# Groups of 384 queries instead of 256 in a block-sparse attention with a gated convolution behind it

## The chip, the core and the metric

The kernel runs on one core of a Trainium2 chip. The time is device time of one execution in microseconds; lower is better. The core has a matrix engine (TensorE, PE in the profile, with its weight loads as PEld), a vector engine (DVE), an activation engine (ACT), a general engine (POOL) and a queue engine (SyncE, SP), which here issues nearly all DMAs. Each works through its own list in order and waits at semaphores.

## The reference

Four batches, eight heads, 768 positions, 64 numbers a head, all float32. A query sees the keys less than 16 positions away and, for each of the 24 blocks of 32 keys, one summary: the maximum of the keys and the mean of the values.

```python
k_sum = k.reshape(B, H, nb, block, D).max(axis=3)
v_sum = v.reshape(B, H, nb, block, D).mean(axis=3)
scores_l = scale * np.matmul(q, k.transpose(0, 1, 3, 2))
mask_l = np.abs(pos[:, None] - pos[None, :]) < window
scores_s = scale * np.einsum('bhsd,bhnd->bhsn', q, k_sum) + np.log(block)
a = softmax over both, with 1e-9 added to the sum
x = np.matmul(a, np.concatenate([v, v_sum], axis=2))       # heads side by side: 768 x 512
gate = sigmoid(sum over k of conv_w[k] * x shifted by k)   # causal, five taps
out = (gate * (x @ w_val)) @ w_out                         # two 512 x 512 matrices
```

## The kernel before

**Tiles and units.** Queries are taken in tiles of 64. A unit is one pair of heads and four such tiles (TPU), a group is the four units (four head pairs) of 256 queries (SG), and there are three groups (NTH) to a batch: 12 groups, 48 units. For a tile, 120 columns of keys stand side by side: 96 positions of the window and 24 block maxima; `v` has the same 120 rows, 96 from the window of `v` (three DMAs, L114) and 24 block means (`vs`, four DMAs of copies out of `vs`, `fill_vs`, L173).

**Stages of a unit.** `stage_s`: scores on PE (`s`, L293), mask and row maximum on DVE (L305), exponentials on ACT (`p`, L316). `stage_n`: reciprocal of the sums on DVE (`ri`), product on POOL (L328). `stage_t`: transposes on PE into one PSUM tile (`pt`, L337) and one copy on ACT (`pts`, L339). `stage_av`: product with `v` on PE (`x`, L351), copies on ACT (`xh` rounded for a fast matmul, `xf` whole), the rest `xl` on POOL, and the five taps of the convolution into PSUM on DVE (`g`, L377; the fifth tap on ACT, L370, in the early groups), then tanh on ACT (`gt`).

**Projections of a group.** `proj_val` (L397) multiplies x by w_val in three fast matmuls for each pair of 128-blocks (high by high, high by low, low by high); group 0, whose weights are not split yet, uses full float32 (L390). DVE gates the result (`gf`, L405), ACT and POOL split it into `gh` and `gl`, and `proj_out` (L419) multiplies by w_out, again in three; ACT scales it into `ob` and SP stores it. Weights and the convolution's coefficients come as 64-bit words and are made into float32 by ACT and DVE (`to_f32`, L186 to L193) and split by ACT and POOL (L228, L229).

**The order of the work.** The program goes by steps, one for each unit. In step s it writes the side work (loads, block maxima `ks` of the next batch's keys on DVE, sums of its values on POOL), then `stage_n` of unit s-1, `stage_av` of unit s-4, `stage_t` of unit s-3 and `stage_s` of unit s (LAG_N, LAG_AV, LAG_T), with pieces of the projections between them as PROJ_RATE allows. SP's list keeps this order; the lists of PE, DVE, ACT and POOL are set by a scheduler when the program is built, PE's from the fifth step on. Tables say at which step of a batch the next batch's keys are loaded (LOAD_K) and reduced (PREP_K), and in which order the first loads go out (LOADS). The keys have eight buffers, `v` and `q` two each. Each DMA takes the next of eight counters in turn, and its issue waits until the DMA eight places before it, the last user of that counter, has landed.

Of the kernel before, what the change touches and what calls it, by code (L numbers as in the profile page):

```python
# [52 lines left out]
def tile_attention_then_gated_conv(  # L53
# [56 lines left out]
    def load_v(g):  # L110
        b, th = divmod(g, NTH)
        t = ld.tile([KW, TPU, DM], F32, tag="v", name=f"v_{g}")
        for r0, r1, s0 in ((0, WIN, 0), (OFF_O, OFF_B, WIN), (OFF_N, KW, WIN + QT)):
            nc.sync.dma_start(t[r0:r1], vw[b, th, s0 : s0 + r1 - r0])  # L114
# [51 lines left out]
    def fill_vs(g):  # L166
        b = g // NTH
        src = vsum[b]
        vr = vtile[g].rearrange("p (t e) c -> p e t c", e=2)
        for e in range(2):  # L170
            for half in range(2):
                off = OFF_A if (e == half) else OFF_B
                nc.sync.dma_start(  # L173
                    vr[off : off + HB, e],
                    src[half * HB : half * HB + HB].unsqueeze(1).broadcast_to([HB, TPU // 2, DM]),
                )
# [156 lines left out]
    def stage_t(u):  # L333
        s = st[u]
        pt = ps_t.tile([P, TPU, P], F32, tag="pt", name=f"pt_{u}")
        for i in range(TPU):
            nc.tensor.transpose(pt[:KW, i, :], s["pn"][:, i, :], ident)  # L337
# [1 line left out]
        nc.scalar.copy(pts, pt[:KW])  # L339
# [42 lines left out]
    def proj_val(g, co):  # L382
# [5 lines left out]
        if g == 0:  # L388
            for ci in range(4):
                nc.tensor.matmul(  # L390
                    pp[:, :SG], wvf[:, ci, cs], G["xf"][:, ci, HALO:],
# [194 lines left out]
```

## Time and profile before

| | |
|---|---|
| median of 3 runs | 293.86 us (293.66 to 294.35) |
| the profiled execution, its time and its span | 295.11 us, 293.3 us |
| PE, DVE, ACT, POOL busy | 250.3, 218.0, 190.1, 155.0 us |
| mean granted TensorE clock | 0.971 |
| DMA | 43.46 MB, 47.7% of the 16 engines' time by the one queue of SP |

In the profile, "L351 x" is the operation of line 351 that writes tile x. A group's row gives count, busy time, mean ns of one, and the idle time before it with what ended it. In a row of the timeline or chain the first two numbers are start and length in us; "SPq" is SP's queue issuing a DMA, "DMA v<-vs" a DMA in flight. Records of PE's matmuls overlap, so their busy time is longer than what they cost back to back. A row of a stage gives its bounds and length, each engine's busy time, the granted clock, the DMA engines' busy share and GB/s.

### The profile page before, as it was taken

To read this page: it belongs to the slowest core of one execution; us is meant where nothing else is said; L and a number is where in the kernel's file an instruction comes from. 1 tells how busy PE (TensorE), PEld (TensorE's weight loads), DVE (VectorE), ACT (ScalarE), POOL (GpSimd) and SP (SyncE) were. 2 spreads that over 40 slices of the span, in tenths; PEclk is the share of its full clock that TensorE was granted. 3 is DMA by queue.
4 is the path that set the end of the run, shared out by engine and by line. 5 is a ranking of instruction groups with operands and counts; after the bars stand their busy time and mean duration, and the time that the engine had idled before them with its cause. 6 is when DMAs were issued, how large, how long until landed. Compare 5 with 4: busy or idle time off the path is not lost.

```text
span 293.3 us, 7550 instructions
## 1 busy us (share of the span) xinstructions
PE 250.3 (85%) x2592; PEld 200.8 (68%) x2592; DVE 218.0 (74%) x827; ACT 190.1 (65%) x686; POOL 155.0 (53%) x224
## 2 busy tenths in 40 slices
PE   1352856999989998979989889699999999999994
PEld 0231634677767775867766677589888887989893
DVE  1948789988679857756749988587898897876420
ACT  1436868857966975947955978377695877735231
POOL 0124346998677666455467578264465453723240
PEclk9999995599999999999999999979999999999999
DMA  7999690781484283660474476706335052202011
GB/s 221 385 242 303 177 368 4 211 305 55 111 254 160 70 207 125 165 200 3 116 235 169 133 235 172 230 0 160 123 104 141 2 152 93 75 0 75 0 74 72
DMA packets 15302, 43.46 MB, mean 148 GB/s; under 512 B 2592, under 2 KB 3360, under 8 KB 14112
## 3 DMA queue, kind: packets, MB, share of 16 engines
q1 hardware_dynamic: 15264, 42.98, 47.7%
q8 instruction: 21, 0.34, 0.5%
q14 instruction: 17, 0.14, 0.2%
HBM read 34.32 MB, written 6.29 MB: 138 GB/s over the span
## 4 chain that ended last, share of the span: by engine, by line
PE 43%; DMA 22%; SPq 13%; DVE 10%; ACT 7%; issue 2%; ACTq 0%
PE val L397 15%; PE out L419 13%; DMA k<-in_kT_dram 12%; SPq L173 7%; PE x L351 7%; PE s L293 4%; PE pt L337 4%; DMA v<-in_vw_dram 3%; DMA v<-vs 3%; SPq L114 3%; DVE g L377 3%; DMA qbd<-in_qT_dram 3%; ACT p L316 3%; DVE ks L121 2%; DVE k L131 2%
## 5 line engine op out<-in xcount | busy, mean ns | idle before, releaser
L377 DVE SCALAR_TENSOR_TENSOR g<-xf,cwt,g 128x256 f32<-128x256 f32 x192 | 93.2, 486 | 7.2 <-ACT g L370 3.7
L316 ACT ACTIVATE p<-sn,nm 128x120 f32<-128x120 f32 x192 | 74.1, 391 | 27.4 <-DVE nm L305 24.3
L397 PE MATMUL val<-xh,wv 128*128 128x256 f32 x352 | 75.2, 296 | 2.2 <-ACT xh L362 1.2
L328 POOL TENSOR_TENSOR p<-p,ri 128x480 f32<-128x480 f32 x48 | 48.5, 1011 | 33.1 <-DVE ri L326 20.9
L397 PEld LDWEIGHTS val<-xh,wv 128*128 128x128 f32 x352 | 57.6, 192 | 6.2 <-ACT xh L362 2.6
L419 PE MATMUL out<-wo,gh 128*128 128x512 f32 x192 | 60.8, 402 | 1.1 <-ACT ob L425 1.1
L365 POOL TENSOR_TENSOR xl<-xf,xh 128x256 fp32r<-128x256 f32 x44 | 32.4, 737 | 41.0 <-ACT xf L363 40.9
L397 PE MATMUL val<-xl,wv 128*128 128x256 f32 x176 | 50.6, 290 | 0.0
L293 PE MATMUL s<-k,qbd 64*64 64x120 f32 x768 | 37.8, 300 | 14.9 <-DVE nm L305 6.1
L407 POOL TENSOR_TENSOR gl<-gf,gh 128x256 fp32r<-128x256 f32 x48 | 35.0, 734 | 22.6 <-ACT gh L406 22.2
L305 DVE CUSTOM_DVE_ANT_0 sn<-s,mask 128x120 f32<-128x120 f32 x192 | 43.7, 275 | 4.2 <-PE s L293 3.9
L293 PEld LDWEIGHTS s<-k,qbd 64*64 64x64 f32 x768 | 23.9, 146 | 26.4 <-issue 11.8
L351 PE MATMUL x<-pts,v 120*64 120x64 f32 x768 | 34.4, 232 | 7.5 <-DMA v<-vs 3.5
L419 PEld LDWEIGHTS out<-wo,gh 128*128 128x128 f32 x192 | 34.2, 188 | 8.4 <-ACT ob L425 1.5
L351 PEld LDWEIGHTS x<-pts,v 120*64 120x64 f32 x768 | 27.3, 140 | 18.1 <-issue 4.6
L337 PE MATMUL pt<-ident,p 128*120 128x128 f32 x192 | 33.3, 299 | 5.3 <-ACT pts L339 3.9
L316 ACT ACTIVATION_READ_ACCUMULATOR p<-sn,nm 128x1 f32 x192 | 37.2, 194 | 0.0
L419 PE MATMUL out<-wo,gl 128*128 128x512 f32 x96 | 37.1, 400 | 0.0
L142 POOL TENSOR_TENSOR vT<-vT 128x384 f32<-128x384 f32 (+3 forms) x48 | 27.4, 577 | 18.1 <-DMA vT<-in_vT_dram 16.7
L397 PEld LDWEIGHTS val<-xl,wv 128*128 128x128 f32 x176 | 33.8, 192 | 1.0 <-issue 0.5
L380 ACT ACTIVATE gt<-g 128x256 f32<-128x256 f32 x48 | 18.7, 389 | 22.4 <-DVE g L377 22.1
L405 DVE SCALAR_TENSOR_TENSOR gf<-gt,val 128x256 f32<-128x256 f32 x48 | 19.7, 417 | 15.3 <-PE val L397 13.1
(44 smaller groups left out, 300.8 us busy)
## 6 DMA issues: line engine op xcount, KB each, us to landing
k<-in_kT_dram SPq DMA_DIRECT2D x16, 478.0 KB
vT<-in_vT_dram SPq DMA_DIRECT2D x16, 384.0 KB
v<-in_vw_dram SPq DMA_DIRECT2D x12, 512.0 KB
out_dram<-ob SPq DMA_DIRECT2D x24, 256.0 KB
qbd<-in_qT_dram SPq DMA_DIRECT2D x11, 512.0 KB
v<-in_vw_dram SPq DMA_DIRECT2D x24, 128.0 KB
v<-vs SPq DMA_DIRECT2D x48, 48.0 KB
raw_wv<-in_wv_dram SPq DMA_DIRECT2D x4, 512.0 KB
```

What stands on the lines that cost most here:

```text
L142: nc.gpsimd.tensor_tensor(dst, src[:, :, :n], src[:, :, n : 2 * n], ALU.add)
L293: nc.tensor.matmul(sp[64 * e : 64 * e + 64, h, j * KW : j * KW + KW], qbd[g % NQB][64 * h : 64 * h + 64, pr, i * QT : i * QT + QT], ktile[ ...
L305: nc.vector.tensor_tensor_reduce(sn[:, n, :], sp[:, h, j * KW : j * KW + KW], mask[:, mv, :], -1.0 / math.sqrt(D), 3.0e38, ALU.add, ALU.mi ...
L316: nc.scalar.activation(p[:, n, :], sn[:, n, :], AF.Exp, bias=nm[:, n : n + 1], scale=-1.0, accum_out=rs[:, n : n + 1],)
L328: nc.gpsimd.tensor_tensor(pn, s["p"], ri.unsqueeze(2).broadcast_to([P, TPU, KW]), ALU.mult)
L337: nc.tensor.transpose(pt[:KW, i, :], s["pn"][:, i, :], ident)
L351: nc.tensor.matmul(xp[h * D : (h + 1) * D, i * QT : (i + 1) * QT], v[:, i, c0 : c0 + D], s["pts"][:, 2 * (i // 2) + h, (i % 2) * QT : (i % ...
L365: nc.gpsimd.tensor_tensor(G["xl"][:, pr, :], x[:, pr, c0 : c0 + SG], G["xh"][:, pr, :].bitcast(F32), ALU.subtract)
L377: nc.vector.scalar_tensor_tensor(gt, x[:, pr, o : o + SG], cwt[:, pr, k : k + 1], gt, ALU.mult, ALU.add)
L397: nc.tensor.matmul(pp[:, :SG], w[:, ci, cs], G[x][:, ci, :], start=(n == 0), stop=(n == 11))
L407: nc.gpsimd.tensor_tensor(G["gl"][:, co, :], gf, G["gh"][:, co, :].bitcast(F32), ALU.subtract)
L419: nc.tensor.matmul(pp, G[gx][:, ci, si * P : si * P + P], w[:, ci, :], start=(n == 0), stop=(n == 11))
```

## The change

A group has 384 queries and a unit six tiles: NTH goes from 3 to 2, so there are 8 groups and 32 units. Each operation of a unit is half as wide again (128x384 for 128x256) or has six pieces for four. `stage_t` is written in two halves of three tiles, each with its own use of the one PSUM tile and its own copy, with a piece of the projections between the halves; the lags become 1, 2 and 3. PROJ_RATE and VAL_COST are half as large again, and the tables of steps are new. Buffers are shared: the keys of all pairs have six buffers under one name, with two of batch 0's value tiles in them; the float32 w_val lies in the buffers of `xh` and `xl`, the float32 w_out in those of `ob`; p, nm, rs, ri and pts have fewer. `v` is laid out in pieces of two tiles, 4096 bytes each, three to a row. The block means of group 0 are issued by ACT instead of SP.

```diff
-NTH = 3
+NTH = 2
+VP = TPU // 2
-LAG_N, LAG_T, LAG_AV = 1, 3, 4
-PROJ_RATE = 1.015
-VAL_COST, OUT_COST = 1.32, 2.6
-ACT_TAP_G = 5
-LOADS = "k0 q0 m k1 q1 n0 i k2 q2 n1 k3 q3 n2 n3 v0 c w0 w1 Q w2 w3"
+LAG_N, LAG_T, LAG_AV = 1, 2, 3
+PROJ_RATE = 1.52
+VAL_COST, OUT_COST = 1.98, 2.6
+ACT_TAP_G = 3
+LOADS = "k0 q0 m k1 q1 n0 i k2 q2 n1 k3 q3 n2 n3 v0 c w0 w1 w2 w3 Q"
-LOAD_K = ((6, 7, 8, 9), (1, 2, 8, 4))
-PREP_K = ((9, 10, 11, 11), (5, 8, 9, 8))
+LOAD_K = ((3, 4, 5, 6), (1, 2, 5, 6))
+PREP_K = ((5, 6, 7, 7), (3, 4, 7, 7))
...
     def load_k(b, pr):
-        t = ld.tile([P, KALLOC], F32, tag=f"k{pr}", name=f"k_{b}_{pr}")
+        t = ld.tile([P, KALLOC], F32, tag="k", name=f"k_{b}_{pr}", bufs=6)
...
-            nc.sync.dma_start(t[r0:r1], vw[b, th, s0 : s0 + r1 - r0])
+            src = vw[b, th, :, s0 : s0 + r1 - r0].rearrange("e r t c -> r e t c")
+            nc.sync.dma_start(t[r0:r1].rearrange("r (e t) c -> r e t c", e=VP), src)
...
     def fill_vs(g):
+        eng = nc.sync if g else nc.scalar
...
-                nc.sync.dma_start(
+                eng.dma_start(
...
-    wvf = cpool.tile([P, 4, DM], F32, tag="wvf", name="wvf")
+    wvf = [wk.tile([P, 2, DM], F32, tag=t, name=f"wvf_{t}") for t in ("xh", "xl")]
...
-            wof[k] = wk.tile([P, DM], F32, tag="wst", name=f"wst_{k}", bufs=2)
+            wof[k] = wk.tile([P, DM], F32, tag="ob", name=f"wst_{k}", bufs=2)
...
-        p = wk.tile([P, TPU, KW], F32, tag="p", name=f"p_{u}", bufs=4)
+        p = wk.tile([P, TPU, KW], F32, tag="p", name=f"p_{u}", bufs=3)
...
-    def stage_t(u):
+    def stage_t(u, half):
         s = st[u]
-        pt = ps_t.tile([P, TPU, P], F32, tag="pt", name=f"pt_{u}")
-        for i in range(TPU):
-            nc.tensor.transpose(pt[:KW, i, :], s["pn"][:, i, :], ident)
-        pts = wk.tile([KW, TPU, P], F32, tag="pts", name=f"pts_{u}", bufs=3)
-        nc.scalar.copy(pts, pt[:KW])
-        s["pts"] = pts
+        n = TPU // 2
+        if half == 0:
+            s["pts"] = wk.tile([KW, TPU, P], F32, tag="pts", name=f"pts_{u}", bufs=2)
+        pt = ps_t.tile([P, n, P], F32, tag="pt", name=f"pt_{u}_{half}")
+        for i in range(n):
+            nc.tensor.transpose(pt[:KW, i, :], s["pn"][:, half * n + i, :], ident)
+        nc.scalar.copy(s["pts"][:, half * n : half * n + n], pt[:KW])
...
+            if 0 <= s - LAG_T < NU:
+                stage_t(s - LAG_T, 0)
             carry = run_proj(carry + PROJ_RATE) if queue else 0.0
             if 0 <= s - LAG_T < NU:
-                stage_t(s - LAG_T)
+                stage_t(s - LAG_T, 1)
```

Three places of the lists show how the work moves. The rows name the line, the operation, what is written and read (tile names with a number, v_112 is group 0's `v`, v_304 group 1's), the shape, and the semaphores waited for; "DMAHW5" is one of the eight DMA counters. First ACT's list around the block means `vs` of group 0, before:

```order
L163 ACTIVATE vs_262<-vsp_257 24x512 [waits PE_49]
L316 ACTIVATE p_227,rs_229<-sn_226,nm_228 128x120 [waits DVE_49] x2
L339 COPY pts_285<-pt_280 120x512 [waits PE_49]
L186 ACTIVATE sc_cw<-cwraw 128x20 [waits DMAHW1_49]
L186 ACTIVATE sc_wv_137<-raw_wv_122 128x512 [waits DMAHW2_49]
```

and now:

```order
L190 ACTIVATE sc_wv_138<-raw_wv_123 128x512 [waits DMAHW2_49]
L166 ACTIVATE vs_298<-vsp_293 24x512 [waits PE_49]
L320 ACTIVATE p_255,rs_257<-sn_254,nm_256 128x120 [waits DVE_49] x3
L177 DMA v_112<-vs_298 12x3x512 [waits Activation_49]
L190 ACTIVATE sc_wv_143<-raw_wv_125 128x512 [waits DMAHW3_49]
L320 ACTIVATE p_255,rs_257<-sn_254,nm_256 128x120 [waits DVE_49] x3
L177 DMA v_112<-vs_298 12x3x512 [waits DMAHW5_49]
L177 DMA v_112<-vs_298 12x3x512 [waits DMAHW7_49]
L190 ACTIVATE sc_wv_148<-raw_wv_129 128x512 [waits DVE_49]
L177 DMA v_112<-vs_298 12x3x512 [waits DMAHW1_49]
L190 ACTIVATE sc_wv_191<-raw_wv_127 128x512 [waits DMAHW4_49,DVE_49,Activation_49]
L368 COPY xf_336<-x_322 128x384 [waits PE_49]
```

Four DMAs now stand in ACT's list between `vs` and the first copy of x, and three of them wait for a DMA counter. Which DMA stands behind a counter is seen in SP's list at that place, now (raw_wv_129 is the last weight, qbd_82 the second q, k_0_312 the first key tile of batch 1):

```order
L204 DMA raw_wv_129<-in_wv_dram 128x1024 [waits DMAHW5_49]
L99 DMA qbd_82<-in_qT_dram 128x1536 [waits DMAHW6_49]
L116 DMA v_304<-in_vw_dram 16x3x1024 [waits DMAHW7_49]
L116 DMA v_304<-in_vw_dram 64x3x1024 [waits DMAHW0_49]
L116 DMA v_304<-in_vw_dram 16x3x1024 [waits DMAHW1_49]
L177 DMA v_304<-vs_298 12x3x512 [waits DMAHW3_49,Activation_49]
L177 DMA v_304<-vs_298 12x3x512 [waits DMAHW4_49]
L177 DMA v_304<-vs_298 12x3x512 [waits DMAHW6_49]
L177 DMA v_304<-vs_298 12x3x512 [waits DMAHW0_49]
L103 DMA k_0_312<-in_kT_dram 128x956 [waits DMAHW2_49,DVE_49]
```

A DMA that waits for a counter takes that counter itself. So ACT's last three DMAs come behind the last weight (5) and the first and third piece of group 1's `v` (7 and 1), and k_0_312 comes behind ACT's first (2). Before, group 1's `v` was issued after all four copies of `vs` into group 0's.

Third, SP's list where a batch's first group is loaded, before (group 3, v_807):

```order
L114 DMA v_807<-in_vw_dram 16x2048 [waits DMAHW7_49,PE_49]
L114 DMA v_807<-in_vw_dram 64x2048 [waits DMAHW0_49]
L114 DMA v_807<-in_vw_dram 16x2048
L173 DMA v_807<-vs_836 12x2x512 [waits DMAHW2_49,Activation_49]
L173 DMA v_807<-vs_836 12x2x512 [waits DMAHW3_49]
L173 DMA v_807<-vs_836 12x2x512 [waits DMAHW4_49]
L173 DMA v_807<-vs_836 12x2x512 [waits DMAHW5_49]
L98 DMA qbd_81<-in_qT_dram 128x1024 [waits DMAHW6_49]
L426 DMA out_dram<-ob_0_924 128x512 [waits DMAHW7_49]
L426 DMA out_dram<-ob_1_968 128x512 [waits DMAHW0_49]
L102 DMA k_0_1002<-in_kT_dram 128x956 [waits DMAHW1_49]
```

and now (group 2, v_665):

```order
L116 DMA v_665<-in_vw_dram 16x3x1024 [waits DMAHW7_49,PE_49]
L116 DMA v_665<-in_vw_dram 64x3x1024 [waits DMAHW0_49]
L116 DMA v_665<-in_vw_dram 16x3x1024 [waits DMAHW1_49]
L177 DMA v_665<-vs_694 12x3x512 [waits DMAHW2_49,Activation_49]
L177 DMA v_665<-vs_694 12x3x512 [waits DMAHW3_49]
L177 DMA v_665<-vs_694 12x3x512 [waits DMAHW4_49]
L177 DMA v_665<-vs_694 12x3x512 [waits DMAHW5_49]
L99 DMA qbd_82<-in_qT_dram 128x1536 [waits DMAHW6_49,PE_49]
L103 DMA k_0_891<-in_kT_dram 128x956 [waits DMAHW7_49]
L108 DMA vT_0_893<-in_vT_dram 128x768 [waits DMAHW0_49,Pool_49]
L431 DMA out_dram<-ob_0_908 128x512 [waits DMAHW1_49,Activation_49]
```

The PE that the first row waits for is the last x of the group whose buffer is taken over. That x is written in the same step as the load before (step 4g+3 for both), and one step earlier now (4g+2). The rest of the list at this place is as it was, but for the stores, which come behind the first key tile.

More of the change, by code (lines that the diff above doesn't have):

```diff
@@ L38 @@
 HALO = NK - 1
+VP = TPU // 2
 REBIAS = 2.0 ** ((127 - 1023) // 8)
-LAG_N, LAG_T, LAG_AV = 1, 3, 4
-PROJ_RATE = 1.015
-VAL_COST, OUT_COST = 1.32, 2.6
-ACT_TAP_G = 5
-LOADS = "k0 q0 m k1 q1 n0 i k2 q2 n1 k3 q3 n2 n3 v0 c w0 w1 Q w2 w3"
-CONVERT = {"wv": (0, 0, 1, 0), "wo": (6, 9, 6, 11)}
-SPLIT = {"wv": (12, 4, 10, 5), "wo": (12, 9, 12, 12)}
-LOAD_K = ((6, 7, 8, 9), (1, 2, 8, 4))
-PREP_K = ((9, 10, 11, 11), (5, 8, 9, 8))
+LAG_N, LAG_T, LAG_AV = 1, 2, 3
[3 more added lines that the diff above has]
+LOADS = "k0 q0 m k1 q1 n0 i k2 q2 n1 k3 q3 n2 n3 v0 c w0 w1 w2 w3 Q"
+CONVERT = {"wv": (0, 0, 1, 0), "wo": (6, 7, 6, 6)}
+SPLIT = {"wv": (8, 3, 7, 4), "wo": (8, 7, 8, 8)}
+LOAD_K = ((3, 4, 5, 6), (1, 2, 5, 6))
+PREP_K = ((5, 6, 7, 7), (3, 4, 7, 7))
 PREP_V0 = (1, 2, 3, 3)
@@ L146, in load_vT0 @@
     def load_vT0(i):
-        t = ld.tile([P, S], F32, tag=f"k{i}", name=f"vT_0_{i}")
+        tag, n = (("k", 6), ("vT", 2))[i // 2]
+        t = ld.tile([P, S], F32, tag=tag, name=f"vT_0_{i}", bufs=n)
         nc.sync.dma_start(t, vT[0, i])
@@ L207, in staged @@
         if nm == "wv":
-            return wvf[:, k]
+            return wvf[k // 2][:, k % 2]
         if k not in wof:
-            wof[k] = wk.tile([P, DM], F32, tag="wst", name=f"wst_{k}", bufs=2)
+            wof[k] = wk.tile([P, DM], F32, tag="ob", name=f"wst_{k}", bufs=2)
         return wof[k]
@@ L284, in stage_s @@
         sn = wk.tile([P, TPU, KW], F32, tag="sn", name=f"sn_{u}")
-        p = wk.tile([P, TPU, KW], F32, tag="p", name=f"p_{u}", bufs=4)
-        nm = wk.tile([P, TPU], F32, tag="nm", name=f"nm_{u}", bufs=10)
-        rs = wk.tile([P, TPU], F32, tag="rs", name=f"rs_{u}", bufs=10)
-        for j in range(2):
+        p = wk.tile([P, TPU, KW], F32, tag="p", name=f"p_{u}", bufs=3)
+        nm = wk.tile([P, TPU], F32, tag="nm", name=f"nm_{u}", bufs=4)
+        rs = wk.tile([P, TPU], F32, tag="rs", name=f"rs_{u}", bufs=4)
+        for j in range(TPU // 2):
             for e in range(2):
@@ L299, in stage_s @@
                     )
-        for j in range(2):
+        for j in range(TPU // 2):
             for h in range(2):
@@ L323, in stage_n @@
         s = st[u]
-        ri = wk.tile([P, TPU], F32, tag="ri", name=f"ri_{u}", bufs=10)
+        ri = wk.tile([P, TPU], F32, tag="ri", name=f"ri_{u}", bufs=4)
         nc.vector.tensor_scalar(ri, s["rs"], 1e-9, None, ALU.add)
@@ L390, in proj_val @@
                 nc.tensor.matmul(
-                    pp[:, :SG], wvf[:, ci, cs], G["xf"][:, ci, HALO:],
+                    pp[:, :SG], wvf[ci // 2][:, ci % 2, cs], G["xf"][:, ci, HALO:],
                     start=(ci == 0), stop=(ci == 3),
@@ L534, in _layout @@
     vn[:, WIN : WIN + S] = v.transpose(0, 2, 1, 3).reshape(B, S, DM)
-    vw = np.zeros((B, NTH, QT + 2 * WIN, TPU, DM), f)
+    vw = np.zeros((B, NTH, VP, QT + 2 * WIN, 2, DM), f)
     for t in range(NT):
-        vw[:, t // TPU, :, t % TPU] = vn[:, t * QT : t * QT + QT + 2 * WIN]
+        i = t % TPU
+        vw[:, t // TPU, i // 2, :, i % 2] = vn[:, t * QT : t * QT + QT + 2 * WIN]
     cw = moe_conv_w.reshape(NK, NPR, 2 * D).transpose(2, 1, 0).reshape(2 * D, NPR * NK)
```

## The prediction

> **What bounds the kernel now.** I read the busy shares first, then three stages, then the chain of waits. Span and engines:
>
> ```profile
> core 0 of [0], span 293.3 us
> PE 250.3 (85%) x2592; PEld 200.8 (68%) x2592; DVE 218.0 (74%) x827; ACT 190.1 (65%) x686; POOL 155.0 (53%) x224
> ```
>
> Busy PE time counts overlapping records, so I price PE by what back-to-back matmuls take in the chain and in the timeline (start, us, line, count):
>
> ```profile
> 226.93 0.62 PE x L351 x16
> 231.93 0.57 PE s L293 x16
> 254.56 0.58 PE pt L337 x4
> 229.88 1.44 PE val L397 x12
> 222.27 4.11 PE out L419 x18
> 39.28 1.56 PE L390 MATMUL val<-xf,wvf 128*128 128x256 f32 x6 [1.85 <-ACT xf L363]
> ```
>
> One record each: x 0.039, s 0.036, pt 0.145, val 0.12, out 0.228, fp32 val 0.26. The program has 768, 768, 192, 528, 288 and 32 of them (counts of the groups): 29.8 + 27.4 + 27.8 + 63.4 + 65.8 + 8.3, with 1.6 for 16 small transposes 224.1 us. The last matmul ends near 289.3, so PE loses about 65 us. Where, the stage view says (length, busy of PE, PEld, DVE, ACT, POOL, clock, DMA share, GB/s), with s, pt, x and fp32 val before 60 us under it:
>
> ```profile
> 0.00:60.00 60.00, 33.54 (x295) 23.05 (x297) 45.36 (x162) 35.26 (x120) 25.98 (x31) 0.89 0.77 241
> 60.00:200.00 140.00, 127.57 (x1421) 101.82 (x1421) 108.04 (x437) 100.62 (x378) 89.04 (x139) 0.99 0.50 154
> 200.00:289.30 89.30, 89.22 (x881) 75.88 (x879) 64.63 (x229) 53.39 (x189) 40.03 (x54) 1.00 0.27 78
> 0.00:60.00 60.00, 9.90 (x160) 0.89 0.77 241
> 0.00:60.00 60.00, 7.32 (x32) 0.89 0.77 241
> 0.00:60.00 60.00, 3.95 (x66) 0.89 0.77 241
> 0.00:60.00 60.00, 12.06 (x32) 0.89 0.77 241
> ```
>
> Before 60: 5.7 + 4.6 + 2.6 + 8.3 + 0.6 = 21.8 us of work, 38 lost. From 200 on PE is full. Between them 224.1 - 21.8 - 89.3 = 113 of 140: 27 lost. So the kernel is a slow start, a middle with gaps, and a PE-bound end.
>
> The start, in the DMA rates of the first 30 us, the timeline and the chain:
>
> ```profile
> 0.00:10.00 10.00, 1.39 (x24) 1.05 (x28) 3.74 (x15) 2.27 (x6) 0.32 (x5) 1.00 0.80 269
> 10.00:20.00 10.00, 5.18 (x56) 2.95 (x48) 7.42 (x31) 4.45 (x22) 1.97 (x2) 1.00 1.05 277
> 20.00:30.00 10.00, 3.17 (x24) 2.11 (x24) 6.87 (x29) 5.58 (x17) 4.88 (x4) 1.00 0.99 310
> 4.05 0.95 DVE L121 TENSOR_REDUCE ks<-k 128x24 f32<-128x768 f32 x1 [4.05 <-DMA k<-in_kT_dram]
> 20.10 3.47 SPq L173 DMA_DIRECT2D v<-vs  x4
> 21.13 9.10 DMA v<-vs
> 31.73 0.91 PE L351 MATMUL x<-pts,v 120*64 120x64 f32 x12
> 33.53 0.49 DVE L377 SCALAR_TENSOR_TENSOR g<-xf,cwt,g 128x256 f32<-128x256 f32 x1 [0.23 <-ACT g L370]
> 59.94 0.69 PE L351 MATMUL x<-pts,v 120*64 120x64 f32 x16
> ```
>
> The means of group 0 are issued at 20.1, land 9 us later behind the weights, and hold the first x; its convolution starts at 33.5, and the fifth x runs at 59.94.
>
> The middle, in SP's waits and one turn of the chain:
>
> ```profile
> SPq L114 <- PE x L351: 116.5, 10, 16.8
> 99.02 0.64 PE x L351 x16
> 100.06 0.61 SPq L114
> 101.33 0.87 SPq L173
> 104.72 0.51 SPq L98
> 105.28 5.40 DMA k<-in_kT_dram
> 110.70 0.95 DVE ks L121
> 116.98 0.71 PE x L351 x16
> ```
>
> SP stands at a group's v load until the last x of two groups ago, then issues v, four means and q, and only then the k that DVE is about to reduce: 99.66 to 110.68, 11 us from x to the landed k. A q or a k stands so in the chain six times between 60 and 200 (from 81.49, 105.28, 123.29, 149.67, 167.98, 181.84): 27 / 6 = 4.5 us of PE lost at each.
>
> **The change part by part.** *PE work.* Per column val costs 0.12/256 and out 0.228/512; the line between gives 0.174 us at 384. 336 x 0.174 = 58.5 against 63.4: -4.9. Group 0 stays fp32 and is half as wide again: 32 x 0.39 against 8.3: +4.2. s, x, pt and out do the same count. Total 223.4: **-0.7**.
>
> *Helpers.* The rows are two sizes each for DVE and ACT, then from the chain one of the three operations of a weight's conversion and one S of a tile on DVE, and from the waits PE's for the copy of transposes:
>
> ```profile
> L377 DVE SCALAR_TENSOR_TENSOR g<-xf,cwt,g 128x256 f32<-128x256 f32 x192 | 93.2, 486 | 7.2 <-ACT g L370 3.7
> L405 DVE SCALAR_TENSOR_TENSOR gf<-gt,val 128x256 f32<-128x256 f32 x48 | 19.7, 417 | 15.3 <-PE val L397 13.1 <-POOL gl L407 1.0 <-POOL xf L273 0.4
> L190 DVE SCALAR_TENSOR_TENSOR wvf<-raw_wv,wvf 128x512 uint32<-128x512 uint32 x4 | 2.8, 691 | 0.0
> L363 ACT COPY xf<-x 128x256 f32<-128x256 f32 x48 | 18.0, 375 | 0.1
> L339 ACT COPY pts<-pt 120x512 f32<-120x512 f32 x48 | 28.2, 588 | 2.4 <-PE pt L337 2.2
> 39.66 0.70 DVE wst L190
> 41.68 0.19 DVE sn L305
> PE pt L337 <- ACT pts L339: 3.9, 3, 3.1
> ```
>
> DVE: (691 - 417)/256 = 1.07 ns a column, so 486 becomes 0.62 us. 128 x 0.62 against 93.2 is -14; gf, ri and the fifth tap give about -8: DVE near 196. ACT: (588 - 375)/256 = 0.83 ns, so 375 becomes 0.48; six copies or casts a unit save some 13 us over 32 units, the transposes in halves give 64 x 0.48 - 28.2 = +2.5 back. None of it is on the path while PE or the loads set the pace; it is slack, priced at 0, and worth up to what the middle loses.
>
> *Start.* Everything up to the weights and the second q is 7552 KB before (sizes of the issue list); with q of 192, v of 1152 and Q of 768 KB, and v_1 behind them, it is 9600 KB = 9.8 MB after. The three windows moved 8.56 MB by 30 us; 1.27 MB more at 310 is 4.1: v_1 lands at 34. The moved means matter for what they wait for: by the order, ACT's second, third and fourth wait for counters of the last weight, of v_1's first and of its last piece. So the fourth is issued at about 34, not 20, and at the 3 us which a small load takes (k, issued at 0.73, was there at 4.05) the first unit's x runs at **37** instead of 31.7. Queued behind that issue on ACT are two weight casts, xf, the tap, the copies of pt and the exponentials of unit 3; all wait. Four issues at SP's 0.8 are 3 us of ACT, inside that wait. On SP the same v_1 holds its fourth mean, then k_1_0; with 5.4 to land that is 40, and DVE has k_1_0's reduce ahead of unit 0's convolution: 40.5 against 33.5. From there to the fifth x lie, on DVE, three convolutions (4 x 0.62), four S (6 x 0.2), two k (0.95 and the two copies, 1.3), one and a half weight conversions (three operations, some 2.2) and 0.7 of ri: 19 us, at the 0.9 of the time that DVE is busy from 30 to 60, 21; with 3.5 for exponential, p, transpose and copy the fifth x runs near 65. PE work done then: 6.8 + 4.4 + 3.7 + 6.2 + 0.5 = 21.6, as before at 60. So the start costs **+5**. Below, -2 (means land early, the lighter DVE makes up for the rest); above, +12 (x at 40, and the ACT, PE and DVE waits add instead of overlapping).
>
> The page *DMA: Bandwidth & Descriptors* of the Trainium skill says (Queues, rings and completion order) that a DMA engine takes turns between the issuers' rings, so ACT's means pass SP's queued k and vT; its section on issuing engines says that a second issuer only saves issue time. By the first the sum stands; by the second k and vT (862 KB at 310, 2.8 us) go first and it would be about 3 higher. No row here shows a DMA issued by ACT.
>
> *Middle.* The last x of a group now lies one step before the v load instead of in its step. A step is 223.4/32 = 7.0 us, of the 11 that k was late. And only four v loads have k behind them (v_2 to v_5). If lateness and loss go together: 4 x 4.5 x (11 - 7)/11 = 6.5 us lost, the best. Against it: the means of a batch's first group wait for the block means, stores of out stand ahead of k_2_1, and a unit has two trips PE-ACT-PE through one PSUM tile where it had one; at worst the 27 stays. I take the middle, 16: **-11**.
>
> *End.* After the last x 21 val and 36 out remain by the order, 3.7 + 8.2 = 12 us of PE work; five taps (3.1), gt, gf, gh, gl and the copies need about 8. No gap: 0.
>
> Sum on the profiled span: 293.3 + 5 - 0.7 - 11 = 286.6. The median of the runs lies 0.6 above the span (293.86), though the profiled execution itself took 295.11. **Forecast: 287 us**, faster by 2%.
>
> **The rivals.** *ACT held at the start* (slower). The moved means wait for v_1, and everything behind them on ACT with them, ending at the fifth x near 72; the lost lead leaves k as late as now at two of the four places. 293.9 + 12 - 0.7 - 6 = **299**. For it: the waits in the order. Against: DVE has only 45 us of work in the first 60, so there is room to catch up. It decides when the fifth x comes later than about 71, 11 behind.
>
> *Two trips a unit* (no change). ACT is 65% busy and in order; where a gh or an exponential stands before the copy of the first half, PE waits at the second. PE already waited 3.9 us for that copy in all (three times), with one copy a step. The middle then loses 22: 293.9 + 5 - 0.7 - 5 = **293**.
>
> *The start costs nothing.* SP's loads are faster than in the windows or the means are not awaited so late, and the middle loses 10: 293.9 - 0.7 - 17 = **276**. For it: ACT, DVE and POOL all fall further below PE's 7.0 a step.
>
> **How the numbers follow.** Forecast 0.53, ACT held 0.24, two trips 0.11, start free 0.12. The forecast's own range is 280 to 293 (start +2 to +8, middle -6 to -16). The range of 80% reaches to the outer cases, leaving a tenth on each side: 275 to 301. Beyond 0.2% (which this kernel's runs can tell) faster: 0.53 + 0.12 = 0.65; same 0.05, out of two trips; slower 0.24 + 0.06 = 0.30.
>
> **What will show it.** Right: the first x near 37 with ACT idle before it on its own DMA issue; the fifth x near 65; SP's wait at the v load far below 116 us; fewer than six q or k on the chain from 65 to 200; val at 0.17 us apiece; PE full from some 190 on. Wrong start: first x by 32, or the fifth after 71. Wrong middle: as many k on the chain, or "ACT pts" among PE's first waits. If PE's work is much off 223, the pricing by columns is wrong.

## The result, and the profile after

The changed kernel takes **327.49 us** (median of four runs, 324.69 to 329.57), the kernel before 293.76 beside it on the same chip: a ratio of 1.112, 95% interval 1.100 to 1.123. It is 11% slower where 2% faster was forecast, and 26 us above the upper end of the range. (A ratio, here and below, leaves disturbed runs out on both sides and so can differ from that of the medians.) The profiled execution took 329.57 us, its span is 327.6.

The prices of the single operations came out as worked out. Groups of the page (count, busy time, mean ns of one, idle before), then from the timeline (start, us) a run of val and one of the fp32 val:

```profile
L382 DVE SCALAR_TENSOR_TENSOR g<-xf,cwt,g 128x384 f32<-128x384 f32 x128 | 79.4, 620 | 6.7 <-ACT g L375 3.4
L345 ACT COPY pts<-pt 120x384 f32<-120x384 f32 x64 | 31.0, 484 | 27.2 <-PE pt L344 27.2
```

```profile
242.40 2.10 PE val L402 x12
```

```profile
76.42 1.45 PE L395 MATMUL val<-xf,wvf_xl 128*128 128x384 f32 x4
```

So val is 0.175 us apiece and fp32 val 0.36, and PE's work is some 223 us by the counts, as before. What came on top is waiting, and in part a lower clock (last section). The stages of the changed kernel (bounds, length, busy of PE, PEld, DVE, ACT, POOL, clock, DMA share, GB/s), which answer to the prediction's three:

```profile
0.00:60.00 60.00, 22.99 (x255) 14.56 (x255) 35.93 (x129) 26.02 (x92) 17.50 (x24) 1.00 0.82 255
60.00:200.00 140.00, 124.63 (x1191) 92.39 (x1190) 101.03 (x363) 87.98 (x307) 84.02 (x105) 0.95 0.47 145
200.00:290.00 90.00, 83.72 (x761) 67.09 (x755) 50.25 (x193) 56.85 (x208) 34.55 (x34) 0.94 0.25 69
```

Busy time is too kind to PE, so for every kernel here I counted the matmuls that began in a stage, line by line, and multiplied by the prices (s 0.036, x 0.039, pt 0.144, out 0.228, val 0.119 at 256 and 0.175 at 384, fp32 val 0.26 and 0.36). What is left of the stage is lost:

| PE time lost, us | 0 to 60 | 60 to 200 | 200 to 290 | after 290 |
|---|---|---|---|---|
| before | 38.3 | 25.0 | 3.6 (0.8 of it behind its last matmul, which ends at 289.2) | |
| after | 44.2 | 33.9 | 17.6 | 3.2 to its last matmul, which ends at 322.1 |

The extra 33 us from one last matmul to the other are 6 at the start, 9 in the middle, 15 from 200 to 290 and 3 behind 290. (For before the prediction put the middle at 27, by difference; the count gives 25.)

*Start.* The timelines of PE, of ACT's queue and of two weight casts on ACT, and the chain:

```profile
37.66 0.48 PE L356 MATMUL x<-pts,v 120*64 120x64 f32 x4 [17.78 <-DMA v<-vs]
41.66 1.33 PE L356 MATMUL x<-pts,v 120*64 120x64 f32 x20 [3.51 <-DMA v<-vs]
71.81 0.84 PE L356 MATMUL x<-pts,v 120*64 120x64 f32 x10
```

```profile
25.00 1.40 ACTq L177 DMA_DIRECT2D v<-vs  x1
27.65 0.80 ACTq L177 DMA_DIRECT2D v<-vs  x1
32.81 0.79 ACTq L177 DMA_DIRECT2D v<-vs  x1
37.89 0.80 ACTq L177 DMA_DIRECT2D v<-vs  x1
33.65 0.66 ACT L190 ACTIVATE sc_wv<-raw_wv 128x512 f32<-128x512 f32 x1 [5.40 <-DMA v<-in_vw_dram]
38.82 0.66 ACT L190 ACTIVATE sc_wv<-raw_wv 128x512 f32<-128x512 f32 x1 [4.51 <-DMA v<-vs]
```

```profile
22.64 14.79 DMA v<-in_vw_dram
37.45 0.78 SPq L177
38.33 5.94 DMA k<-in_kT_dram
44.30 0.96 DVE ks L123
```

v_1's last piece lands at 37.4, ACT's fourth mean leaves right behind it, the rest of the first x runs at 41.7 and the fifth x at 71.8; before they were at 31.7 and 59.9. Two weight casts in ACT's list stood behind its third and fourth DMA for 9.9 us. (The profiled execution of the kernel before is a late one there: in the seven kernels below that are made from it and leave the first loads and group 0's means in their order, the first x begins at 27.8 to 28.8 us where it begins at 30.3, and the fifth at 56.0 to 58.6.)

*Middle.* One turn of the chain again, from the last x of a group to the landed k:

```profile
104.33 0.62 PE x L356 x14
105.36 0.67 SPq L116
106.71 0.84 SPq L177
...
110.70 8.27 DMA k<-in_kT_dram
118.99 0.95 DVE ks L123
...
139.44 0.62 PE x L356 x14
140.46 0.67 SPq L116
141.19 7.06 DMA v<-in_vw_dram
148.31 5.71 DMA k<-in_kT_dram
```

It takes 14.0 us where it took 11: 1.2 MB of v (0.8 before) are loaded ahead of k, and in the first turn 0.8 MB of q (0.5 before). The waits that stood out:

```profile
DVE ks L123 <- DMA k<-in_kT_dram: 27.3, 8, 5.8
ACT ob L430 <- DMA out_dram<-ob: 17.7, 5, 5.8
SPq L116 <- PE x L356: 92.8, 6, 26.5
```

SP stands 15.5 us at each v load where it stood 11.7, with a group half as long again. Of DVE's wait for k 6 us lie ahead of 10 us in both kernels; from 60 us on it is 20.7 us and was 10.0.

*End.* The chain and PE's timeline at 212 to 227:

```profile
212.92 0.67 SPq L116
214.33 0.82 SPq L177
...
218.30 7.50 DMA out_dram<-ob
225.82 0.61 ACT ob L430
```

```profile
226.47 1.22 PE L424 MATMUL out<-wo,gh 128*128 128x512 f32 x2 [2.91 <-ACT ob L430]
```

A group now has three stores of out and still two tiles for them. The stores stand on SP behind the v load, which waits for an x, and behind its means; then they fly together with v and q for 7.5 us. ACT's copy waits for the tile, and PE for ACT. At 253.6 the same happens once more.

### The profile page after: what moved, and what is told of

Read it like the earlier page. It is cut to its first block, busy times and chain, and to the rows that moved or that the text cites. A ratio compares the mean times of both kernels' runs of the same rounds, so it can differ in the third digit from the quotient of the medians.

```text
span 327.6 us, 6755 instructions
## 1 busy us (share of the span) xinstructions
PE 262.1 (80%) x2400; PEld 198.9 (61%) x2400; DVE 201.2 (61%) x707; ACT 183.2 (56%) x630; POOL 146.7 (45%) x172
## 4 chain that ended last, share of the span: by engine, by line
PE 37%; DMA 29%; DVE 13%; ACT 7%; SPq 5%; POOL 5%; issue 3%; ACTq 0%; POOLq 0%
PE out L424 15%; DMA v<-in_vw_dram 12%; DMA k<-in_kT_dram 10%; PE val L402 9%; DVE g L382 5%; PE x L356 5%; DMA out_dram<-ob 4%; PE pt L344 4%; ACT p L320 3%; PE s L297 3%; SPq L177 2%; DMA vT<-in_vT_dram 2%; DVE sn L309 2%; SPq L116 2%; DVE ks L123 2%
## 5 line engine op out<-in xcount | busy, mean ns | idle before, releaser
L332 POOL TENSOR_TENSOR p<-p,ri 128x720 f32<-128x720 f32 x32 | 44.9, 1404 | 90.4 <-DVE ri L330 63.9
L382 DVE SCALAR_TENSOR_TENSOR g<-xf,cwt,g 128x384 f32<-128x384 f32 x128 | 79.4, 620 | 6.7 <-ACT g L375 3.4
L402 PE MATMUL val<-xh,wv 128*128 128x384 f32 x224 | 65.7, 355 | 8.7 <-ACT ob L430 6.0
L402 PEld LDWEIGHTS val<-xh,wv 128*128 128x128 f32 x224 | 41.4, 192 | 13.3 <-ACT ob L430 7.6
L345 ACT COPY pts<-pt 120x384 f32<-120x384 f32 x64 | 31.0, 484 | 27.2 <-PE pt L344 27.2
L297 PE MATMUL s<-k,qbd 64*64 64x120 f32 x768 | 37.3, 294 | 10.9 <-DVE k L133 5.2
L424 PEld LDWEIGHTS out<-wo,gh 128*128 128x128 f32 x192 | 36.9, 197 | 14.9 <-DVE gf L410 3.5
L412 POOL TENSOR_TENSOR gl<-gf,gh 128x384 fp32r<-128x384 f32 x32 | 32.0, 1010 | 26.9 <-ACT gh L411 26.9
L402 PE MATMUL val<-xl,wv 128*128 128x384 f32 x112 | 39.8, 355 | 1.7 <-POOL xl L370 1.6
L370 POOL TENSOR_TENSOR xl<-xf,xh 128x384 fp32r<-128x384 f32 x28 | 28.2, 1007 | 22.1 <-ACT xf L368 22.1
L329 DVE TENSOR_SCALAR ri<-rs 128x6 f32<-128x6 f32 x32 | 7.5, 235 | 39.8 <-ACT p L320 39.8
L123 DVE TENSOR_REDUCE ks<-k 128x24 f32<-128x768 f32 x16 | 15.1, 946 | 27.3 <-DMA k<-in_kT_dram 27.3
```

The costliest lines, as they stand in the source:

```text
L297: nc.tensor.matmul(sp[64 * e : 64 * e + 64, h, j * KW : j * KW + KW], qbd[g % NQB][64 * h : 64 * h + 64, pr, i * QT : i * QT + QT], ktile[ ...
L332: nc.gpsimd.tensor_tensor(pn, s["p"], ri.unsqueeze(2).broadcast_to([P, TPU, KW]), ALU.mult)
L345: nc.scalar.copy(s["pts"][:, half * n : half * n + n], pt[:KW])
L370: nc.gpsimd.tensor_tensor(G["xl"][:, pr, :], x[:, pr, c0 : c0 + SG], G["xh"][:, pr, :].bitcast(F32), ALU.subtract)
L382: nc.vector.scalar_tensor_tensor(gt, x[:, pr, o : o + SG], cwt[:, pr, k : k + 1], gt, ALU.mult, ALU.add)
L402: nc.tensor.matmul(pp[:, :SG], w[:, ci, cs], G[x][:, ci, :], start=(n == 0), stop=(n == 11))
```

## The experiments

Each verdict gives the median and the ratio to the kernel before, which ran beside it (medians 293.2 to 294.3 us). An edit can make the scheduler (the planner of the expectations) put PE, DVE, ACT and POOL in another order, so the run that measures this alone comes first.

### Another order, nothing else

```diff
-PROJ_RATE = 1.015
+PROJ_RATE = 1.03
```

> The kernel before with only the rate at which projections are let in raised from 1.015 to 1.03: the same instructions and loads, in another order on PE, DVE, ACT and POOL. If the order that the planner finds is worth as much as the parts, the time moves by 3 us or more in either direction, and effects of that size (v's pieces, six k buffers, stores) can't be put down to their part; if it stays within 1.5 us of 293.8, they can.

291.8 us, ratio 1.005 (0.999 to 1.011). So this other order moved the time by 1% at most, and below I put nothing smaller down to a part. It is one order of many: how far another would move the time is not known, so an effect of 2 or 3% is not safely the part's either.

### The start

In the changed kernel, the means by SP again:

```diff
-        eng = nc.sync if g else nc.scalar
+        eng = nc.sync
```

> One part undone: group 0's block means are issued by SP again, ahead of v_1, as in the kernel before; all else as changed (327.5 us). Theory 'means behind v_1': the first x comes back from 37.7 to 30-33 us, the fifth x from 71.8 to 60-63, and the run is 9 to 12 us shorter, 316-319. Rival 'larger loads': the start is late because q, v and weights of groups of 384 are half as large again, the fifth x stays after 69 and the time within 3 of 327. Rival 'the lead is given back': the fifth x is early, but later loads are paced by SP, and the time falls by less than half of what the fifth x gains.

**313.96 us**, ratio 1.067 (1.059 to 1.076): 13.5 us, more than any theory gave, from one line. The first x runs at 33.3 and 34.7, the fifth at 66.3, 5.5 us earlier than with ACT and not the 9 to 12 expected; the rest of the gain comes later (28.9 us lost from 60 to 200 instead of 33.9, 14.3 from 200 to 290 instead of 17.6).

The reverse, in the kernel before:

```diff
-                nc.sync.dma_start(
+                (nc.sync if g else nc.scalar).dma_start(
                     vr[off : off + HB, e],
```

> The kernel before (293.7 us) with only group 0's four means issued by ACT instead of SP. Theory 'the queue itself': in the changed kernel undoing this gave 13 us, so here too the fourth mean's issue waits for a piece of v_1, ACT's casts and copies behind it wait, the first x moves from 31.7 to 35-37 and the time is 5 to 12 us longer, 299-306. Rival 'only with the larger v': v_1 is 768 KB here, lands some 4 us sooner, and the time stays within 3 of 293.7.

312.4 us, ratio 1.055 (1.051 to 1.058), more than either theory had. The first x moves to 37.2, the fifth from 59.9 to 67.7, and the delay of 8 us there is 16 at the end by the ratio (24 at the last x of the profiled execution, which was its longest, 316.9). ACT's queue in its timeline:

```profile
21.84 3.30 ACTq L173 DMA_DIRECT2D v<-vs  x2
29.62 0.79 ACTq L173 DMA_DIRECT2D v<-vs  x1
32.11 0.79 ACTq L173 DMA_DIRECT2D v<-vs  x1
```

Is it ACT, or v_1 ahead of the means? In the changed kernel, SP issues all, v_1 first:

```diff
-        eng = nc.sync if g else nc.scalar
+        eng = nc.sync
...
             prep_vs(0)
-            fill_vs(0)
             load_v(1)
+            fill_vs(0)
             fill_vs(1)
```

> The changed kernel with group 0's means issued by SP, but behind v_1's three pieces instead of ahead of them (314.0 us ahead of them, 327.5 by ACT). Theory 'v_1 ahead is what costs': the means are as late as by ACT, first x at 36-40, fifth x at 69-73 and the time is 324-330 although ACT issues nothing. Rival 'ACT is held': ACT's casts and exponentials run on while SP waits, the fifth x is at 66-68 and the time 314-319.

**327.7 us**, ratio 1.117 (1.106 to 1.129): the same as by ACT, with ACT issuing nothing. The order of v_1 and the means decides the time; who issues the means does not show in it. SP's timeline, with the eight means of both groups in one row, and PE's:

```profile
22.21 2.40 SPq L116 DMA_DIRECT2D v<-in_vw_dram  x3
25.69 12.06 SPq L177 DMA_DIRECT2D v<-vs  x8
```

```profile
38.16 0.48 PE L356 MATMUL x<-pts,v 120*64 120x64 f32 x4 [17.87 <-DMA v<-vs]
66.61 0.56 PE L356 MATMUL x<-pts,v 120*64 120x64 f32 x10
```

But the fifth x is at 66.6, 5.2 us earlier than by ACT, as the rival had it: ACT's weight casts no longer stand behind DMAs. That is also where it is with the means first (66.3), and the 13.7 us between these two runs come after it: 33.2 us lost from 60 to 200 against 28.9, and 16.4 against 14.3 from 200 to 290. (The profile of the run with the means first is of an execution of 318.1 us, 4 above its median, so it shows only part of the difference.) How a start that has caught up by the fifth x costs so much later is not settled.

An earlier start than before, in the kernel before (with its last k by ACT, as in a run further down): w_val's third and fourth part behind the means.

```diff
-... v0 c w0 w1 Q w2 w3"
-CONVERT = {"wv": (0, 0, 1, 0), "wo": (6, 9, 6, 11)}
+... v0 c w0 w1 Q"
+CONVERT = {"wv": (0, 0, 4, 4), "wo": (6, 9, 6, 11)}
...
             fill_vs(0)
+            load_w4("wv", wv, (2, 3))
             load_v(1)
```

> The kernel before with the k loads of the third and fourth batch by ACT (289.9 us), and the third and fourth part of wv loaded behind group 0's means instead of ahead of them. Theory 'the means are late behind the weights': they land in 4 to 6 us instead of 9, the first x moves from 31.7 to 28-29, and the time is 285-288. Rival 'DVE and the projections': val of group 0 waits for the weights' conversion, and the time is 290 or more.

302.2 us, ratio 1.023 (1.005 to 1.041), 12 us above the kernel that it is made from. Its first x runs at 26.5 and its fifth at 59.1; in that kernel they run at 27.8 and 56.0. So the first comes 1.3 us earlier, the fifth 3.1 later, and from 60 to 200 it loses 32.8 us against 21.5 there. The edit also converts those two weight parts three and four steps later, so it doesn't show what an early first x is worth by itself. In this run and the last the fifth x does not tell the end: 3.1 us there are 12 at the end, and 0.3 us there are 13.7.

### The end

```diff
-        nc.sync.dma_start(out[b, r0 : r0 + P, :], ob)
+        nc.scalar.dma_start(out[b, r0 : r0 + P, :], ob)
```

In the changed kernel:

> One part added: the 24 stores of out are issued by ACT, right behind the copy that fills the tile, instead of by SP, where they stand behind the v load and its four means. Theory 'stores behind v hold out's two buffers': ACT's wait for out<-ob falls from 17.7 us to under 5, PE is full from 200 us on, and the run is 10 to 20 us shorter, 308-318. Rival 'symptom': the 24 issues on ACT (0.8 us each, 19 us) and other waits eat it, and the time stays within 4 of 327.

323.2 us, ratio 1.097 (1.087 to 1.106). ACT's wait for the tile falls from 17.7 to 4.6 us, and the stage from 200 to 290 loses 9.0 instead of 17.6 us. But the middle loses 37.8 instead of 33.9, and of the 8.6 us 4.3 are left (the intervals of the two ratios, 1.087 to 1.106 and 1.100 to 1.123, overlap):

```profile
60.00:200.00 140.00, 117.64 (x1149) 88.77 (x1150) 98.75 (x356) 89.72 (x313) 81.32 (x99) 0.96 0.49 152
200.00:290.00 90.00, 89.06 (x838) 71.01 (x837) 57.31 (x212) 60.10 (x214) 42.22 (x45) 0.99 0.24 69
```

With the means by SP as well:

> Both together: group 0's means by SP (314.0 us alone) and out's stores by ACT (323.2 alone, 327.5 without). Theory 'two separate losses': they add, 314.0 - 4.3 to 314.0 - 9, so 305-310, because with the means by SP the stage from 200 to 300 us still loses 15 us, and the stores by ACT cut that stage's loss to 8. Rival 'one limit behind both': the middle gives the store's gain back as it did in the run with the stores alone (117.6 instead of 124.6 us of PE busy from 60 to 200), and the time is 312 or more.

313.1 us, ratio 1.066 (1.053 to 1.078): 0.8 below the means alone, so the rival held. Again the stage from 200 loses 7.8 instead of 14.3 us and the middle 31.9 instead of 28.9. The wait behind v is real and local; removing it shortens the whole by no more than the runs can tell. ACT's 24 issues, or the other order that they bring, may be what the middle pays; that was not told apart.

### The middle

With means by SP and stores by ACT, the k loads of the later batches by ACT too:

```diff
-        nc.sync.dma_start(t[:, :KTOT], kT[b, pr])
+        (nc.scalar if b else nc.sync).dma_start(t[:, :KTOT], kT[b, pr])
```

> As the kernel with SP's means and ACT's stores, and the k loads of the second to fourth batch are issued by ACT as well, so that they no longer stand in SP's order behind the v load that waits for the last x of a group. Theory 'k behind v': DVE's waits for k (22.4 us with SP's means) fall under 8, the loss from 60 to 200 us (27 us) shrinks by 8 or more, and the time is 8 to 15 us below the kernel without this edit. Rival 'shared wires': k then lands beside v instead of behind it, both later, and the time moves by less than 3.

310.6 us, ratio 1.064 (1.052 to 1.076). DVE waits 16.4 us for k instead of 29.0, the middle loses 27.3 instead of 31.9, and the start 1.6 more, since ACT issues batch 1's first k at 10.9 us, among the first loads. 2.5 us in all, which the ratios (1.064 and 1.066) don't tell apart: the rival's number, though DVE's wait nearly halved.

In the changed kernel, the block maxima of the next batch later:

```diff
-PREP_K = ((5, 6, 7, 7), (3, 4, 7, 7))
+PREP_K = ((5, 6, 7, 7), (6, 6, 7, 7))
```

> One table changed: from the second batch on, the block maxima of the next batch's k (and the block sums of its v) are done in steps 6, 6, 7, 7 of eight instead of 3, 4, 7, 7, with the loads where they are (1, 2, 5, 6). Theory 'k two steps after its load': DVE's waits for k (27.3 us in all) fall to 10 or less and the stretch from 72 to 200 us loses some 10 us less, 315-320. Rival 'the k waits are covered': DVE's wait falls but the time stays within 3 of 327, since what waits behind it is late for another reason.

328.2 us, ratio 1.115 (1.106 to 1.124): nothing, and DVE's wait for k stays at 27.2. But the edit didn't move what it was to move. The scheduler orders DVE's list, and the reduces are where they were, those of the third batch at 95.2, 98.7, 118.2 and 121.8 us for 96.6, 100.4, 119.0 and 122.5, still right behind their loads and with nearly the same waits, of which two:

```profile
95.24 0.95 DVE L123 TENSOR_REDUCE ks<-k 128x24 f32<-128x768 f32 x1 [4.25 <-DMA k<-in_kT_dram]
118.21 0.95 DVE L123 TENSOR_REDUCE ks<-k 128x24 f32<-128x768 f32 x1 [5.98 <-DMA k<-in_kT_dram]
```

So neither theory was put to the test.

The lags of before in the changed kernel with the means by SP, and the change's lags in the kernel before:

```diff
-LAG_N, LAG_T, LAG_AV = 1, 2, 3
+LAG_N, LAG_T, LAG_AV = 1, 3, 4
```

> Group 0's means by SP, and the lags of transposes and x as in the kernel before, 3 and 4 steps instead of 2 and 3; buffers as changed. Theory 'too little lead': a late k or exponential reaches PE one step earlier with the short lags, and with the long ones the time falls from 314.0 to 304-309. Rival 'SP's order decides': v's load then waits for an x one step later (7 us), k and the stores behind it too, and the time is 316-322.

321.8 us, ratio 1.099 (1.089 to 1.108): 7.8 slower than with the short lags, as the rival had it: SP's wait for x is 109.6 us instead of 86.4.

```diff
-LAG_N, LAG_T, LAG_AV = 1, 3, 4
+LAG_N, LAG_T, LAG_AV = 1, 2, 3
```

> The kernel before (293.9 us) with only its lags shortened from 3 and 4 to 2 and 3 steps. Theory 'a lag of one step less frees v a step earlier' (the prediction's middle): SP's wait at the v load falls from 116 us by some 40, k comes 5 us earlier, and the time is 285-291. Rival 'too little lead': PE waits for transposes, and the time is 297-305.

**301.1 us**, ratio 1.026 (1.014 to 1.037): slower. SP's wait at the v load did fall as the prediction's premise asks, from 116.5 to 99.2 us, but the wait for x gave way to waits behind it and DVE's wait for k stayed (17.3 against 16.5):

```profile
SPq L114 <- PE x L351: 99.2, 9, 16.8
SPq L114 <- PE s L293: 12.9, 1, 12.9
SPq L107 <- POOL vT L142: 13.1, 1, 13.1
```

The middle loses 28.1 instead of 25.0 us. The rival's number came, but not its reason: PE's wait for the copy of the transposes is 1.1 us, and was 3.9. Both kernels are worse by 7 to 9 us with the other's lags.

Does k behind v cost what the prediction put on it? In the kernel before, the k loads of the third and fourth batch by ACT:

```diff
-        nc.sync.dma_start(t[:, :KTOT], kT[b, pr])
+        (nc.scalar if b > 1 else nc.sync).dma_start(t[:, :KTOT], kT[b, pr])
```

> The kernel before with only the k loads of the third and fourth batch issued by ACT, so that they don't stand behind a v load in SP's order. Theory of the prediction 'k behind v is what the middle loses' (27 us at six places, four of them in these batches): 10 to 18 us shorter, 276-284. Rival 'covered by the backlog of projections': DVE's waits for k fall and the time moves by less than 4.

289.9 us, ratio 0.983 (0.978 to 0.988), the fastest kernel of the study, and the only one whose ratio is clearly below 1. DVE's wait for k falls by a third:

```profile
DVE ks L121 <- DMA k<-in_kT_dram: 11.0, 5, 4.1
```

That is 5 us less wait and 4 us less time, not 10 to 18. And it doesn't hold beside other edits. With the stores by ACT as well:

> The kernel before with the k loads of the third and fourth batch and all stores of out issued by ACT. By the theory that out's stores behind v cost only where a group has three of them, nothing beyond the run with the k loads alone (within 2 us). Rival: another 3 to 5 us shorter, since a store behind the v load holds one of out's two buffers here too (ACT waited 4.0 us for it).

295.9 us, ratio 1.003 (0.997 to 1.008). With the order changed on SP instead, k's loads at steps 1, 1, 2, 2:

> The kernel before with the k loads of the third and fourth batch issued by SP at steps 1, 1, 2, 2 of twelve instead of 1, 2, 8, 4, so that two of the four no longer stand right behind a v load. Theory 'k behind v': DVE's waits for k fall from 16.5 us to 10, and the time is 287-291, as with k by ACT. Rival 'order': the waits fall and the time stays within 3 of 293.8 or rises, since another order of the rest decides.

293.1 us, ratio 1.010 (1.005 to 1.016), although DVE's wait for k is down to 7.6 us. So in one version of four (the fourth, with v in pieces, is further down) the lower wait went with a shorter time, by 1.7%, and one reorder alone was worth up to 1%: what k's wait is worth by itself is not shown. Nowhere does it come near the 4.5 us a place of the prediction.

Six shared k buffers in the kernel before:

```diff
-        t = ld.tile([P, KALLOC], F32, tag=f"k{pr}", name=f"k_{b}_{pr}")
+        t = ld.tile([P, KALLOC], F32, tag="k", name=f"k_{b}_{pr}", bufs=6)
...
-LOAD_K = ((6, 7, 8, 9), (1, 2, 8, 4))
-PREP_K = ((9, 10, 11, 11), (5, 8, 9, 8))
+LOAD_K = ((8, 9, 9, 10), (1, 2, 9, 10))
+PREP_K = ((10, 11, 11, 11), (5, 8, 11, 11))
```

> The kernel before with only its k buffers shared as in the change, six instead of eight, so that the third and fourth k of the next batch can be loaded only when the first two of this batch are used up; its load and prepare tables are set for that (loads 8, 9, 9, 10 and 1, 2, 9, 10 of twelve steps, maxima 10, 11, 11, 11 and 5, 8, 11, 11). Theory 'shared k buffers cost': k comes at the last moment, DVE's waits for k rise from 16.5 to 25 us or more, and the time is 298-306. Rival 'six are enough': within 3 of 293.7, and the loss of the changed kernel's middle lies in its units and lags.

297.4 us, ratio 1.011 (1.006 to 1.016), at the edge of what a reorder does, and DVE's wait for k is 14.9 us, not 25: six are nearly enough.

### The pieces of v

In the changed kernel, v in whole rows again (vw as [B, NTH, 96, TPU, DM], one row of 12288 bytes for three of 4096):

> One part undone: v lies in memory as whole rows of six tiles (12288 bytes) instead of three pieces of 4096; all else as changed. Theory 'pieces cost': the v load, 7.1 to 7.3 us from issue to landing in the chain, comes down to under 6.3, the loads and stores behind it move up as much, and the run is 3 to 8 us shorter. Rival 'bytes count': the landing stays at 7 us and the time within 2 of 327.

331.1 us, ratio 1.128 (1.121 to 1.135), against 1.112 (1.100 to 1.123): the intervals touch. The pieces don't slow v; whether they help isn't shown. In the kernel before, with the last k by ACT:

> The kernel before with the k loads of the third and fourth batch by ACT (289.9 us) and v in pieces of 4096 bytes as in the change. If the pieces spread v over more queues, a further 1 to 4 us, 286-289; if they only helped the larger v, within 1.5 of 289.9.

291.8 us, ratio 1.000 (0.995 to 1.005). No gain, and that of k by ACT is not there either, with DVE's wait for k at 11.7 us.

### All parts but the units

The kernel before with the means by ACT, lags 1, 2, 3, six k buffers and the pieces of v: the edits above together.

> The kernel before with all parts of the change except the units of six tiles and the buffers that go with them: group 0's means by ACT (alone +18 us), lags of 2 and 3 (alone +7.4), six shared k buffers with late loads (alone +3.1), v in pieces of 4096 bytes (undone in the change +3.6, so -3 here). If the parts add, 294.3 + 25.5 = 320 and the units themselves cost some 8 more. Rival 'they overlap': the late start hides the others' cost, the time is 309-314, and the units of six cost 14 to 18. Rival 'they multiply': 326 or more, and the units cost nothing.

**305.0 us**, ratio 1.042 (1.032 to 1.052). The parts overlap: 12 us together, less than the means alone (16 by the ratio). Its first x runs at 32.8, not 37.2, and from 200 to 290 it loses 4.6 us, where the kernel before loses 3.6. So 20 to 22 of the 33 us are added only when the units of six tiles come in, with what goes with them (the wider loads, three stores on two tiles, fewer p, pts and nm buffers, the tables of steps). Of these only the stores were taken out alone, and they gave 0.8 to 4.3 us; which of the rest it is stays open. From the other side it is the same: with the means by SP and the stores and later k by ACT, the changed kernel still takes 310.6 us, 17 more than the kernel before.

## Why the prediction was wrong, point by point

**PE's work, -0.7.** Right: some 223 us by the counts against 223.4; val 0.175 instead of 0.174, fp32 val 0.36 instead of 0.39.

**Helpers, 0.** The durations were right (620 and 484 ns for 0.62 and 0.48; DVE 201 us for 196). That their slack was "worth up to what the middle loses" was not: all three engines fell to 45 to 61% busy and the middle lost more.

**Start, +5.** That the means wait for v_1 was right, the size was not, and it was already wrong at the first convolution: 47.2 instead of 40.5, about as much as the 6.8 us by which the fifth x missed 65. Two terms failed. v_1's last 1.27 MB were put at 310 GB/s; the stretch in which they were nearly alone in flight moved 134:

```profile
30.00:40.00 10.00, 0.48 (x4) 0.32 (x4) 1.61 (x4) 1.84 (x4) 0.67 (x1) 1.00 0.68 134
```

so v_1 landed at 37.4, not 34, and k took 5.9 us, not 5.4. And from the landed k to the convolution I counted 0.5 us, where DVE's timeline has the reduce and two copies, 2.9 from 44.27 to 47.18:

```profile
44.30 0.95 DVE L123 TENSOR_REDUCE ks<-k 128x24 f32<-128x768 f32 x1 [0.41 <-DMA k<-in_kT_dram]
45.28 1.97 DVE L133 COPY k<-ks 128x84 f32<-128x84 f32 x2
47.18 2.59 DVE L382 SCALAR_TENSOR_TENSOR g<-xf,cwt,g 128x384 f32<-128x384 f32 x4
```

Counted at the fifth x the start cost 12 us; undone, 13.5. That these two agree says little: by SP in the same place the fifth x came 5.2 us earlier and the time was the same. What the late means cost is shown by its end, 13.5 us; the way from there to the end is open.

**Middle, -11.** Wrong in sign: 8.9 us more lost. The step that failed is "a step is 7.0 us, of the 11 that k was late": those 7 us were not won. x, v and k move together: SP still waits for an x at each of the six v loads that take over a buffer, from the x to the landed k it is 14.0 us now, and from 60 us on DVE waits 20.7 us for k instead of 10.0. The shorter distance from LOAD_K to PREP_K does not show in the runs: in both kernels DVE's list has the reduces of the third and fourth batch right behind their loads, 4.5 to 6.8 us after the issue before and 5.5 to 8.4 now. The other half of that step, "4.5 us of PE lost at each", took a wait on the chain for its price: with DVE's wait down by a third and by a half the time moved by -1.7% and +1.0%. On the chain between 60 and 200 there are three k and no q now, half of the six, as forecast; fewer entries on the chain did not mean less time. What a later k costs PE, no run separates from the other parts of the larger unit.

**End, 0.** Wrong: 17.6 us lost between 200 and 290 where the kernel before loses 3.6. The prediction looked for a gap behind the last x, and missed that three stores share two tiles behind SP's v load. Taken out, that stage's loss fell by 6.5 to 8.6 us, and the time by 0.8 to 4.3.

**The rivals.** "ACT held at the start" had the right condition (the fifth x after 71: 71.8) and the right price for the start (12). Its mechanism is there at the start: ACT's weight casts stood for 9.9 us, and without ACT's issues the fifth x comes at 66.6. It doesn't make the time, which is the same with ACT issuing nothing and v_1 ahead. Its 299 still counted 6 us of gain in the middle and nothing at the end. What I took from the Trainium skill's page *DMA: Bandwidth & Descriptors* (Issuing engines are not separate DMA queues), that a second issuer only saves issue time, agrees with this (327.7 us by SP, 327.5 by ACT). "Two trips a unit" has no trace: from 66 us on PE waited 0.4 us in all for the copy of the transposes. "The start costs nothing" fell with the first x.

**The range.** Its upper end, 301, was a sum of small terms with one of them at its worst. The end, which I priced at nothing, lost 18 us more than before (15 up to 290, 3 behind it), over half of the whole, and a wait can cost PE's clock as well (below).

## What to carry to other kernels

A DMA that waits for one of a few counters takes its place in the order of all loads, so a small one on the way to the first result has to stand ahead of the large ones, whichever engine issues it. When units grow, look for every buffer pair that a group passes through more often than before (here three stores on two tiles), and don't price a chain entry by the wait beside it: take the wait away in a run first. Where a scheduler orders the engines, measure a mere reorder before any effect of 1% is believed, and look in the trace whether an edit moved what it was to move.
